# Preparing attention two pairs ahead, with tiny gate matmuls, a three-matmul inverse DFT and v by a plain DMA, in a fused attention and Hyena kernel

## The chip, the cores and the metric

The kernel runs on one core of a Trainium2 chip. The metric is the device time of one execution in microseconds (us). All runs quoted are fast runs, unless a run is called slow. The engines of a profile are PE (TensorE, matmuls), PEld (weight loads of PE), DVE (VectorE), ACT (ScalarE), POOL (GpSimd) and SP (the engine that issues most DMAs here). In the profile's lines L193 is line 193 of that kernel, x6 means six instructions, and `out<-in` names what is written and read. The granted clock is the share of PE's full clock that PE got; "half clock" is a stretch at 0.50.

## The reference

Block-sparse attention (4 batches, 8 heads, 768 positions, 64 numbers per head), and then a Hyena block on its output. Cut to what matters:

```python
# attention: each query sees its own 64-block and the 3 blocks with the best gate score, causally
k_rep = k.reshape(B, H, 12, 64, D).mean(axis=3)
gate_scores = einsum('bhsd,bhnd->bhsn', q, k_rep)      # causal blocks only
sel = top3(gate_scores) | own_block
attn = softmax(where(sel & causal, q @ k.T / sqrt(D), -1e9))
x = (attn @ v) as [B, S, 512]
# Hyena block
x1, x2, x3 = split(x @ w_proj)                          # 512 -> 3 * 512
conv = irfft(rfft(x2) * rfft(filter_fft))               # along the 768 positions
out = (x1 * conv * x3) @ w_out
```

## The kernel before

Heads are taken in pairs, four pairs in a batch. For each pair a *preparation* transposes q and k (`qp`, `kp`), forms the block means of k (`ks`), the gate scores and from them a mask (`ms`), and copies the parts by DMA into the operands `Qt` and `Kt` of the score matmuls. The mask lies in rows 64 to 75 of `Qt`, so a score can't start before the mask's DMA has landed. Attention of batch b runs together with the Hyena block of batch b−1. The Hyena block of the last batch runs alone, which this text calls the tail.

Loads and preparation of one pair:

```python
def load_v(st, j):                 # POOL issues it; the DMA converts fp32 to fp16
    for t in range(2):
        nc.gpsimd.dma_start(st["va"][:, :, 2 * j + t, 0:D], v_r[st["b"], :, :, 2 * j + t, :])

def pair_gen(st, j):
    ...  # qp -> q2h, q2l ; Qt[0:64] by DMA ; kp -> k2, ks ; Kt[0:64] by DMA
    for t in range(2):             # block means as a sum of two fp16 numbers
        nc.vector.tensor_copy(kmh[i][r, j, cc], ks[r, :])
        nc.vector.tensor_tensor(kml[i][r, j, cc], ks[r, :], kmh[i][r, j, cc], op=ALU.subtract)
```

Gates: wide matmuls with the means as weights, a copy by ACT, and fp32 transposes back.

```python
def gate_gen(st, j0, jn):          # batch 0: pair by pair; later batches: four pairs at once
    for part in range(2):
        for (wt, src) in ((kmh, q2h), (kml, q2h), (kmh, q2l), (kml, q2l)):
            for j in range(j0, j0 + jn):
                nc.tensor.matmul(gt[32*j:32*j+32, 0:w], lhsT=wt[:, j, :], rhs=src[:, j, P+p0:P+p0+w], ...)
        nc.scalar.copy(gts[gr, p0:p0 + w], gt[gr, 0:w])
    ...                            # transposes gts -> gn, top 3, mask nm, mt, ms
    nc.sync.dma_start(Qt[...][64:76, h % 2, P:S], ms[...])
```

Filter, frequency product and inverse DFT:

```python
def filter_gen():                  # runs within batch 0
    nc.gpsimd.dma_start(wp, ...); nc.gpsimd.dma_start(wo, ...)     # weights
    yield from trig_back()
    ...                            # six loads f0, f1 by SP, then fe = f0 + f1 (POOL), fo = f0 - f1 (DVE)

# in hyena_gen, for each block c of frequencies:
nc.gpsimd.tensor_sub(Y[:, c, 0, :], t1, t2)
nc.gpsimd.tensor_add(Y[:, c, 1, :], t3, t4)
# inverse DFT, for each dc and parity: two matmuls of 128 rows and two of 64
terms = [(Y[:, par, kk, ds_], G[:, 2 * par + kk, :]) for kk in range(2)]
terms += [(Y[r, 2, kk, ds_], G[r, 4 + kk, :]) for kk in range(2)]    # r: 64 rows
```

Order of the work: pair 0 is prepared first, and the instruction streams are then merged by weight.

```python
load_qk(st, 0); load_qk(st, 1)
for j in range(NP): load_v(st, j)
merge([first_pair, trig_gen])
# batch 0: attention, pairs 1..3, filter, and all four pairs of batch 1
# batch 1, 2: attention, Hyena of the batch before, all four pairs of the next batch
# batch 3: attention, Hyena ; then the tail
```

The softmax here doesn't subtract the row's maximum and nothing guards it: scores larger than these inputs give would overflow.

Of the kernel before, what the change touches and what calls it, by code (L numbers as in the profile page):

```python
# [17 lines left out]
def kernel(  # L18
# [25 lines left out]
    MAGIC = float(2 ** 23)  # L44
    TWO_PI = 2.0 * math.pi
# [33 lines left out]
    nc.gpsimd.tensor_copy(id16, id32)  # L79

    NS = 6
    Kt, Qt, kmh, kml = [], [], [], []
    for i in range(NS):
        Kt.append(const.tile([P, 2, S], FP16, name=f"Kt{i}"))
        Qt.append(const.tile([P, 2, S], FP16, name=f"Qt{i}"))
    for i in range(2):
        kh_ = const.tile([P, NP, 32], FP16, name=f"kmh{i}")
        kl_ = const.tile([P, NP, 32], FP16, name=f"kml{i}")
        nc.gpsimd.memset(kh_, 0.0)
        nc.gpsimd.memset(kl_, 0.0)  # L90
        kmh.append(kh_)
        kml.append(kl_)
    for i in range(NS):
        nc.vector.memset(Qt[i][64:P, :, :], 0.0)
# [7 lines left out]
    nc.gpsimd.memset(rowv, 1.0)  # L102
    nc.gpsimd.iota(rowv[0:1, :], pattern=[[1, HS]], base=0, channel_multiplier=0,
                   allow_small_or_imprecise_dtypes=True)
    cv3 = colv.rearrange("p (g k n) -> p g k n", g=3, k=2)
    nc.gpsimd.memset(cv3[:, :, 0, :], COS)
    nc.gpsimd.memset(cv3[:, :, 1, :], SIN)
    nc.gpsimd.memset(colv[:, P:P + 1], COS)
    nc.gpsimd.iota(cv3[0:1, 0:2, :, :], pattern=[[1, 2], [0, 2], [2, P]], base=0, channel_multiplier=0,
                   allow_small_or_imprecise_dtypes=True)  # L110
    nc.gpsimd.iota(colv[0:1, 2 * 256:S], pattern=[[0, 2], [1, 2], [2, 64]], base=256, channel_multiplier=0,  # L111
                   allow_small_or_imprecise_dtypes=True)
    nc.gpsimd.memset(colv[0:1, P:P + 1], 384.0)


    eblk = const.tile([P, S], FP16)
    nc.gpsimd.memset(eblk, 0.0)
    nc.gpsimd.memset(eblk[64:76, :], EMASK)
    nc.gpsimd.affine_select(
        out=eblk[64:76, :], in_=eblk[64:76, :], compare_op=ALU.is_ge,  # L120
        fill=0.0, base=0, pattern=[[1, S]], channel_multiplier=-64)
    nc.gpsimd.affine_select(
        out=eblk[64:76, :], in_=eblk[64:76, :], compare_op=ALU.is_ge,
        fill=0.0, base=63, pattern=[[-1, S]], channel_multiplier=64)
# [40 lines left out]
    def dft_fwd(xe, xo, c, kind, pt):  # L165

        if c < 2:
            src = xe if c == 0 else xo
            col = 256 * c + 128 * kind
            for t in range(HC):  # L170
                nc.tensor.matmul(pt, lhsT=F[:, t, col:col + P], rhs=src[:, t, :],
                                 start=(t == 0), stop=(t == HC - 1))
        else:
            col = 512 + 128 * kind
            for t in range(HC):
                for r, src in ((0, xe), (64, xo)):
                    nc.tensor.matmul(pt[r:r + 64, :], lhsT=F[:, t, col + r:col + r + 64],
                                     rhs=src[:, t, :], start=(t == 0), stop=(t == HC - 1),
                                     skip_group_check=True)

    def filter_gen():
        nc.gpsimd.dma_start(wp, moe_w_proj.rearrange("(c p) n -> p c n", p=P))
        nc.gpsimd.dma_start(wo, moe_w_out.rearrange("(c p) n -> p c n", p=P))
        yield 0.1
# [11 lines left out]
        for t, (f0, f1) in enumerate(fs):  # L196
            nc.gpsimd.tensor_tensor(fe[:, t, :], f0, f1, op=ALU.add)
            nc.vector.tensor_tensor(fo[:, t, :], f0, f1, op=ALU.subtract)
            yield 0.3
        for c in range(HC):  # L200
# [12 lines left out]
    q_r = q.rearrange("b h (c p) d -> b p c h d", p=P)  # L213
    k_r = k.rearrange("b h (c p) d -> b p c h d", p=P)
    v_r = v.rearrange("b h (c p) d -> b p c h d", p=P)

    def prep_begin(b):
        va = gp.tile([P, NQ, H, 65], FP16, name="va", tag="va")
        q2h = gp.tile([P, NP, S], FP16, name="q2h", tag="q2h", bufs=1)
        q2l = gp.tile([P, NP, S], FP16, name="q2l", tag="q2l", bufs=1)  # L220
        return dict(b=b, i=b % 2, va=va, q2h=q2h, q2l=q2l)

    def load_qk(st, j):
        b = st["b"]
        qn = nat.tile([P, NQ, 2, D], FP32, name="qn", tag="qn")
        kn = nat.tile([P, NQ, 2, D], FP32, name="kn", tag="kn")
        for t in range(2):
            nc.sync.dma_start(qn[:, :, t, :], q_r[b, :, :, 2 * j + t, :])
        for t in range(2):
            nc.sync.dma_start(kn[:, :, t, :], k_r[b, :, :, 2 * j + t, :])  # L230
        st[("n", j)] = (qn, kn)

    def load_v(st, j):
        if j == 0:
            nc.gpsimd.memset(st["va"][:, :, :, 64:65], 1.0)
        for t in range(2):
            nc.gpsimd.dma_start(st["va"][:, :, 2 * j + t, 0:D], v_r[st["b"], :, :, 2 * j + t, :])  # L237

    def pair_gen(st, j):
        i = st["i"]  # L240
        sl = (NP * st["b"] + j) % NS
        qn, kn = st[("n", j)]
        q2h, q2l = st["q2h"], st["q2l"]
        for hf in range(2):
            cs = slice(HS * hf, HS * (hf + 1))
            qp = ms_tile("qp")
            for c in range(HC):
                nc.tensor.transpose(qp[:, P * c:P * (c + 1)], qn[:, HC * hf + c, :, :], id32)  # L248
            nc.scalar.activation(q2h[:, j, cs], qp[:, 0:HS], AF.Copy, bias=0.0, scale=QS)  # L249
            nc.vector.scalar_tensor_tensor(out=q2l[:, j, cs], in0=qp[:, 0:HS], scalar=QS,  # L250
                                           in1=q2h[:, j, cs], op0=ALU.mult, op1=ALU.subtract)
            yield 0.33
        for t in range(2):
            nc.sync.dma_start(Qt[sl][0:64, t, :], q2h[64 * t:64 * t + 64, j, :])
        k2 = qkT.tile([P, S], FP16, name="k2", tag="k2")
        ks = qkT.tile([P, NB], FP32, name="ks", tag="ks")
        for hf in range(2):
            cs = slice(HS * hf, HS * (hf + 1))
            kp = ms_tile("kp")
            for c in range(HC):  # L260
                nc.tensor.transpose(kp[:, P * c:P * (c + 1)], kn[:, HC * hf + c, :, :], id32)  # L261
            nc.scalar.copy(k2[:, cs], kp[:, 0:HS])  # L262
            nc.vector.reduce_sum(ks[:, 6 * hf:6 * hf + 6],  # L263
                                 kp[:, 0:HS].rearrange("p (n t) -> p n t", t=64), axis=AX.X)
            yield 0.33
        for t in range(2):
            nc.sync.dma_start(Kt[sl][0:64, t, :], k2[64 * t:64 * t + 64, :])
        for t in range(2):
            r = slice(64 * t, 64 * t + 64)
            cc = slice(12 * t, 12 * t + 12)  # L270
            nc.vector.tensor_copy(kmh[i][r, j, cc], ks[r, :])
            nc.vector.tensor_tensor(kml[i][r, j, cc], ks[r, :], kmh[i][r, j, cc], op=ALU.subtract)

    W5 = S - P
    GW = (384, 256)

    def gate_gen(st, j0, jn):
        i = st["i"]
        q2h, q2l = st["q2h"], st["q2l"]
        gr = slice(32 * j0, 32 * (j0 + jn))  # L280
        hs = slice(2 * j0, 2 * (j0 + jn))
        gts = gp.tile([P, W5], FP32, name="gts", tag="gts", bufs=1)
        for part in range(2):
            p0, w = 384 * part, GW[part]
            gt = ms_tile("gt")
            n_ = 0
            for (wt, src) in ((kmh[i], q2h), (kml[i], q2h), (kmh[i], q2l), (kml[i], q2l)):
                for j in range(j0, j0 + jn):
                    nc.tensor.matmul(gt[32 * j:32 * j + 32, 0:w], lhsT=wt[:, j, :],  # L289
                                     rhs=src[:, j, P + p0:P + p0 + w],  # L290
                                     start=(n_ == 0), stop=(n_ == 3), skip_group_check=True)
                n_ += 1
            nc.scalar.copy(gts[gr, p0:p0 + w], gt[gr, 0:w])
            yield 0.8
        m8 = gp.tile([P, 5, H, 8], FP32, name="m8", tag="m8")
        nm = gp.tile([P, 5, H, NB], FP16, name="nm", tag="nm")
        for part in range(2):
            c0, cn = (1, 3) if part == 0 else (4, 2)
            gn = ms_tile("gn")
            for c in range(c0, c0 + cn):  # L300
                o = P * (c - c0)
                nc.tensor.transpose(gn[:, o + 32 * j0:o + 32 * (j0 + jn)],
                                    gts[gr, P * (c - 1):P * c], id32[gr, gr])

            gnh = gn.tensor

            def gap(p0, pn, c, cn_, n0, nn, cs=0):

                aps = [[512, pn]]
                if cn_ > 1:  # L310
                    aps.append([P + cs, cn_])
                aps += [[32, jn], [12, 2]]
                if nn > 1:
                    aps.append([1, nn])
                return bass.AP(tensor=gnh, offset=p0 * 512 + P * (c - c0) + 32 * j0 + n0, ap=aps)

            nc.vector.memset(gap(0, 64, c0, cn, 2 * c0 + 1, 1, cs=2), NEG)
            if part == 0:
                nc.vector.memset(gap(0, P, 1, 1, 4, 8), NEG)
# [239 lines left out]
    if True:  # L559
# [51 lines left out]
        for _ in hyena_gen(prev):  # L611
            pass
# [30 lines left out]
```

## Time and profile before

The median is 326.01 us in 3 runs (323.42 to 327.32). The profiled execution has a span of 325.2 us from its first to its last instruction.

The page's slices of the kernel before follow. Each digit is the busy share in one of 40 equal slices, in tenths; PEclk is the granted TensorE clock in tenths; DMA is the mean busy share of the 16 DMA engines.

```profile
PE   3613379687594797899889998999899999899984
PEclk9999998899978999999999999999999999999999
DMA  8999996166669945572009973200230000130005
```

PE has little to do in the first slices, while the DMA engines are busy. After slice 14 PE is nearly full.

The table of busy time by stretch follows, with cuts that I set at the first exp activation of each batch and at the last of all: start, batches 0 to 3, tail, and then the 18 us from 11 to 29 us alone. The columns are: from and to, length, busy time of each engine (with the number of instructions), granted clock, DMA share and GB/s. The DMA share adds up the times of the packets, so it can pass 1 where they overlap.

```profile
0.00:39.69 39.69, 14.08 (x52) 7.62 (x53) 27.65 (x77) 11.63 (x20) 27.10 (x48) 1.00 1.41 201
39.69:111.56 71.87, 54.24 (x480) 35.09 (x479) 39.94 (x203) 40.32 (x66) 16.74 (x33) 0.91 0.83 130
111.56:171.40 59.84, 53.52 (x486) 30.68 (x485) 42.63 (x137) 36.41 (x60) 24.84 (x36) 1.00 0.37 84
171.40:234.30 62.90, 58.65 (x516) 33.76 (x515) 42.52 (x141) 39.89 (x67) 30.77 (x42) 1.00 0.50 91
234.30:280.15 45.85, 45.38 (x388) 24.46 (x386) 26.04 (x53) 31.28 (x45) 22.99 (x33) 1.00 0.10 35
280.15:325.20 45.05, 37.13 (x219) 17.02 (x219) 18.13 (x35) 15.79 (x31) 15.91 (x12) 1.00 0.19 71
11.00:29.00 18.00, 5.99 (x24) 2.96 (x25) 15.33 (x53) 4.45 (x9) 9.05 (x11) 1.00 1.57 206
```

Three regimes are to be seen. In the start (39.7 us) PE works for 14.1 us. In batch 0 PE is busy for 54.2 of 71.9 us. From batch 1 on PE is busy for 89%, 93%, 99% and 82% of the stretch. The line for 11 to 29 us: PE and ACT have little to do there, but the DMA engines move 206 GB/s.

The chain of waits of the kernel before shows why attention starts so late (start, length, what; SPq is SP issuing):

```profile
14.55 3.94 SPq L193
...
19.01 13.72 DMA f_748<-in_moe_filter_fft_dram
...
33.93 4.63 DMA Qt_99<-ms
...
38.61 1.89 PE sp L385 x6
```

A filter load takes 13.7 us, DVE waits for it in `x2o`, the mask copy `ms` is queued behind that, the mask's DMA takes 4.6 us, and the first score `sp` runs at 38.61 us. Later in batch 0 the chain passes through a mask DMA twice more, for 4.3 us at 80.0 and for 3.2 us at 107.6.

Groups of instructions of the kernel before (line, engine, operation, out<-in, forms, count | busy us, mean ns | idle before, and what ended it):

```profile
L511 PE MATMUL cv<-G,Y 128*128 128x384 f16 x64 | 15.7, 327 | 0.7 <-POOL Y L484 0.5
L511 PE MATMUL cv<-G,Y 64*128 64x384 f16 x64 | 15.5, 328 | 0.7 <-POOL Y L484 0.5 <-POOL Y L483 0.2
```

The inverse DFT's matmul takes 328 ns with 64 rows of contraction and 327 ns with 128. Issuing the converting DMAs for v keeps POOL for another 26.9 us (32 issues).

### The profile page before, as it was taken

The numbers are of one execution on the slowest core, as the hardware profiler recorded it, in microseconds if no ns is written. First come the engines' busy times: TensorE is split into PE (matmuls) and PEld (weight loads), VectorE is DVE, ScalarE is ACT, GpSimd is POOL, SyncE is SP. The second block draws the span as 40 slices with busy tenths as digits, with TensorE's granted clock in tenths as the row PEclk, the third lists the DMA queues.
The fourth block names the chain that finished last, engine by engine and source line by source line (L and its number), as shares of the span: only waits on it lengthen the run. The fifth ranks groups of instructions, "written<-read, shape, count | busy, mean of one in ns | idle before, by whom it ended". The sixth has DMA issues, their size and how long they took to land.

```text
span 325.2 us, 6030 instructions
## 1 busy us (share of the span) xinstructions
PE 263.0 (81%) x2134; PEld 148.6 (46%) x2134; DVE 196.9 (61%) x644; ACT 175.3 (54%) x285; POOL 138.3 (43%) x202
## 2 busy tenths in 40 slices
PE   3613379687594797899889998999899999899984
PEld 2202145554362363555444645554455555444431
DVE  7992434768448059977642699685508765429530
ACT  2522367386650595555728866465485666461324
POOL 8924821110118126623339284244216754308540
PEclk9999998899978999999999999999999999999999
DMA  8999996166669945572009973200230000130005
GB/s 172 229 174 245 180 135 133 20 149 145 148 150 185 74 108 139 131 170 40 1 18 240 155 156 84 48 3 6 85 123 1 2 0 2 73 123 1 0 2 194
DMA packets 86558, 32.87 MB, mean 101 GB/s; under 512 B 77184, under 2 KB 82176, under 8 KB 86528
## 3 DMA queue, kind: packets, MB, share of 16 engines
q1 hardware_dynamic: 60384, 27.24, 35.5%
q0 software_dynamic: 26144, 5.25, 20.1%
q8 instruction: 17, 0.28, 0.3%
q14 instruction: 13, 0.11, 0.1%
HBM read 24.64 MB, written 6.29 MB: 95 GB/s over the span
## 4 chain that ended last, share of the span: by engine, by line
PE 53%; DVE 14%; DMA 11%; ACT 8%; POOL 6%; issue 4%; SPq 2%; POOLq 1%; ACTq 0%; DVEq 0%
PE x13p L495 9%; PE sp L385 8%; PE x2p L464 5%; PE cv L511 5%; PE po L403 5%; ACT ex L389 5%; DMA f_748<-in_moe_filter_fft_dram 4%; PE op L524 3%; PE kp L261 3%; PE qp L248 3%; PE gt L289 3%; POOL yT L519 2%; DVE ks L263 2%; PE xp L423 2%; DMA qn<-in_q_dram 2%
## 5 line engine op out<-in xcount | busy, mean ns | idle before, releaser
L389 ACT ACTIVATE ex<-sp 128x1024 f16<-128x1024 f32 (+1 forms) x96 | 85.9, 924 | 27.6 <-PE sp L385 26.8
L391 POOL TENSOR_SCALAR_AFFINE_SELECT ex<-ex 128x256 f16<-128x256 f16 x96 | 39.8, 417 | 114.4 <-ACT ex L389 114.4
L495 PE MATMUL x13p<-xT,wp 128*128 128x384 f16 x256 | 49.0, 326 | 1.7 <-ACT x_2170 L501 0.6
L519 POOL TENSOR_TENSOR yT<-prod,sd 128x768 f16<-128x768 f32 x16 | 29.0, 1810 | 28.2 <-DVE sd L518 25.3
L403 PEld LDWEIGHTS <-ex 128*128 128x128 f16 x672 | 30.8, 99 | 15.4 <-issue 7.6
L403 PE MATMUL po<-va,ex 128*128 128x65 f16 x672 | 36.0, 196 | 1.7 <-PE qp L248 1.5
L495 PEld LDWEIGHTS <-wp 128*128 128x128 f16 x256 | 23.6, 98 | 17.5 <-issue 4.9
L250 DVE SCALAR_TENSOR_TENSOR q2l<-qp,q2h 128x384 f16<-128x384 f32 x32 | 17.2, 550 | 23.0 <-ACT q2h L249 22.6
L511 PE MATMUL cv<-G,Y 128*128 128x384 f16 (+1 forms) x128 | 28.9, 327 | 1.4 <-POOL Y L484 0.9
L249 ACT ACTIVATE q2h<-qp 128x384 f16<-128x384 f32 x32 | 15.7, 496 | 23.0 <-PE qp L248 22.6
L237 POOL DMA_DIRECT2D va<-in_v_dram x32 | 26.9, 861 | 0.0
L524 PE MATMUL op<-wo,yT 128*128 128x512 f16 x96 | 23.2, 380 | 3.9 <-POOL yT L519 3.9
L261 PE MATMUL kp<-id_91,kn 128*128 128x128 f32 x96 | 19.5, 327 | 6.3 <-DVE ms L345 3.4
L248 PE MATMUL qp<-id_91,qn 128*128 128x128 f32 x96 | 18.8, 320 | 7.0 <-DMA qn<-in_q_dram 5.1
L527 ACT COPY osb<-op 128x512 f32<-128x512 f32 x24 | 13.4, 590 | 20.1 <-PE op L524 18.7
L263 DVE TENSOR_REDUCE ks<-kp 128x6 f32<-128x384 f32 x32 | 17.4, 552 | 6.4 <-ACT k_1063 L262 3.8
L415 DVE TENSOR_TENSOR xn<-po,rec 128x384 f16<-128x384 f32 x32 | 17.8, 555 | 0.7
L261 PEld LDWEIGHTS kp<-id_91,kn 128*128 128x128 f32 x96 | 13.0, 167 | 11.2 <-DVE ms L345 3.8
L248 PEld LDWEIGHTS qp<-id_91,qn 128*128 128x128 f32 x96 | 12.6, 161 | 12.0 <-POOL colv L111 5.1
L411 DVE RECIPROCAL rec<-po 128x6 f32<-128x6 f32 x32 | 6.1, 189 | 19.0 <-PE po L403 18.5
L517 DVE TENSOR_TENSOR sd<-ce,cv 128x384 f32<-128x384 f32 x16 | 8.8, 552 | 13.5 <-PE cv L511 11.4
L511 PEld LDWEIGHTS <-Y 128*128 128x128 f16 (+1 forms) x128 | 9.0, 96 | 15.4 <-issue 11.4
(297 smaller groups left out, 489.6 us busy)
## 6 DMA issues: line engine op xcount, KB each, us to landing
qn<-in_q_dram SPq DMA_DIRECT2D x32, 192.0 KB
kn<-in_k_dram SPq DMA_DIRECT2D x32, 192.0 KB
out_dram<-osb SPq DMA_DIRECT2D x24, 256.0 KB
va<-in_v_dram POOLq DMA_DIRECT2D x32, 96.0 KB, 6.2
wp<-in_moe_w_proj_dram POOLq DMA_DIRECT2D x1, 1536.0 KB, 18.9
Qt_99<-q2h SPq DMA_DIRECT2D x6, 96.0 KB
Qt_101<-q2h SPq DMA_DIRECT2D x6, 96.0 KB
Qt_103<-q2h SPq DMA_DIRECT2D x6, 96.0 KB
```

Of the source, the lines that this page charges most:

```text
L237: nc.gpsimd.dma_start(st["va"][:, :, 2 * j + t, 0:D], v_r[st["b"], :, :, 2 * j + t, :])
L248: nc.tensor.transpose(qp[:, P * c:P * (c + 1)], qn[:, HC * hf + c, :, :], id32)
L261: nc.tensor.transpose(kp[:, P * c:P * (c + 1)], kn[:, HC * hf + c, :, :], id32)
L263: nc.vector.reduce_sum(ks[:, 6 * hf:6 * hf + 6], kp[:, 0:HS].rearrange("p (n t) -> p n t", t=64), axis=AX.X)
L385: nc.tensor.matmul(sp[:, col:col + w], lhsT=kt[:, P * kc:P * (kc + 1)], rhs=qt[:, q0:q0 + w], start=True, stop=True, skip_group_check=True)
L389: nc.scalar.activation(ex[:, 0:w], sp[:, 0:w], AF.Exp, scale=ESC)
L391: nc.gpsimd.affine_select(out=dv, in_=dv, compare_op=ALU.is_ge, fill=0.0, base=0, pattern=[[0, 2], [1, P]], channel_multiplier=-1)
L403: nc.tensor.matmul(po[:, 65 * c:65 * c + 65], lhsT=exs[pi][:, col:col + P], rhs=st["va"][:, kc, h, :], start=(kc == 0), stop=(kc == c), sk ...
L495: nc.tensor.matmul(xp[:, 0:HS], lhsT=wp[:, d2, base + P * dc:base + P * (dc + 1)], rhs=xT[:, d2, hs:hs + HS], start=(d2 == 0), stop=(d2 == ...
L511: nc.tensor.matmul(cv[:, 0:HS], lhsT=lh, rhs=rh, start=(n_ == 0), stop=(n_ == 3))
L519: nc.gpsimd.tensor_mul(yT[:, dc, :], prod, sd)
L524: nc.tensor.matmul(op, lhsT=yT[:, d2, P * c:P * (c + 1)], rhs=wo[:, d2, :], start=(d2 == 0), stop=(d2 == DC - 1))
```

## The change

It has five parts: prepare each pair by itself, two pairs ahead of its attention, from the start to the end of the kernel; compute gate scores directly in their natural layout by tiny matmuls; fold the two 64-row terms of the inverse DFT into one of 128 rows; load v as fp32 by a plain DMA from SP and cast it on POOL; and move small set-up work between engines. Cut to its core:

```diff
+    load_qk(0); load_v(0); load_qk(1); load_v(1)
+    merge([Stream(prep_gen(0), ...), Stream(trig_gen(), ...), Stream(prep_gen(1), ...)])
+    for sl in range(2, NS): fill_kt(sl)
+    def later_preps(b):
+        for j in range(NP):
+            g = NP * b + j + AHEAD                  # AHEAD = 2
+            if g < NG:
+                if g + 1 < NG: load_qk(g + 1); load_v(g + 1)
+                yield from prep_gen(g)
+    load_qk(AHEAD); load_v(AHEAD)                   # after the merge above
     ...
-    # gate_gen: wide matmuls, ACT copy, fp32 transposes
+        for c in range(1, NQ):
+            for n_, (qx, w) in enumerate(((q2h, 0), (q2h, 1), (q2l, 0), (q2l, 1))):
+                nc.tensor.matmul(gn[:, 32 * c:32 * c + 24], lhsT=qx[:, P * c:P * (c + 1)],
+                                 rhs=km[:, w, 0:24], start=(n_ == 0), stop=(n_ == 3))
     ...
-        Y = hy.tile([P, HC, 2, Dm], FP16, name="Y", tag="Y")
+        Y = hy.tile([P, 6, Dm], FP16, name="Y", tag="Y")
-            nc.gpsimd.tensor_sub(Y[:, c, 0, :], t1, t2)
-            nc.gpsimd.tensor_add(Y[:, c, 1, :], t3, t4)
+            if c < 2: ...                           # as before
+            else:
+                for par in range(2):
+                    r = slice(64 * par, 64 * par + 64)
+                    nc.gpsimd.tensor_sub(Y[0:64, 3 * par + 2, :], t1[r, :], t2[r, :])
+                    nc.gpsimd.tensor_add(Y[64:P, 3 * par + 2, :], t3[r, :], t4[r, :])
     ...
-                for n_, (lh, rh) in enumerate(terms):                          # 4 terms
+                for n_, g_ in enumerate((2 * par, 2 * par + 1, 4 + par)):      # 3 terms
     ...
-        nc.gpsimd.dma_start(st["va"][...], v_r[...])
+        nc.sync.dma_start(vn, v_r[:, n, :])         # later, on POOL: va = vn in fp16
     ...
+        # filter_gen: the weight loads now come after the filter loads
```

The diff has a sixth part: the changed kernel builds its whole schedule under `tc.manual_schedule(engines={SP, Pool})`, which the kernel before does not. In the changed kernel SP follows the program text, which has the loads of pair 2 after the masks of pairs 0 and 1, and the six filter loads within batch 0. In the kernel before the text has the filter within batch 0, but its trace shows the six loads issued from 6.7 to 19.4 us, in the start.

## The prediction

> **What bounds the kernel now.** The page's slices and a table of busy time by stretch show three regimes. 0–38.6 us: no attention; PE 13.0 us busy, DVE 27.7. 38.6–110 us (batch 0 with seven pair preparations and the filter): PE 77%, ACT 56%, DVE 56%; granted clock 0.90. 110–283 us: PE 88%, 94%, 97%, PE-bound. 283–325 us: the last hyena alone, PE 83%. In the chain of waits the first score waits for a mask DMA (33.9–38.6 us), which waits for a DVE mask copy queued behind a filter operand still loading (19.0–32.7 us). Later scores of batch 0 again wait 4.3 and 3.2 us for a mask DMA: the just-in-time chain transpose, means, gate, mask, DMA, score is exposed.
>
> **What changes, costed from the trace.**
> 1. Start. Only pairs 0 and 1 are prepared before attention; filter loads come later; v is not queued four pairs deep. The new start should be DVE-bound: mask memsets (six of 0.8 us), 18 trig operations (0.35–0.55 us), two preparations, block-row copies; the instruction order puts pair 0's mask copy after nearly all of it. Estimate: first score at 31 us instead of 38.6: −7.5 us.
> 2. Batch 0. Four preparations (pairs 2–5) instead of seven, two pairs ahead, so no score waits for a mask. PE work about 36–40 us, ACT about 34, DVE about 41. Estimate 47 us instead of 71: −24 us. Partly this moves work: two preparations (2 × 3.8 us PE) go to batch 3, whose PE is full: +6 us. Together −18.
> 3. Inverse DFT: 4 matmuls to 3 for each of 32 accumulations. The 64-row and 128-row forms take 328 and 327 ns, and eight take about 1.6 us in the chain, 0.2 us each; so 32 × 0.2–0.27 = 6–8 us less PE. This agrees with the Trainium skill, "TensorE: Matmul & The Clock Gate", LDWEIGHTS section: rows of the contraction don't matter. About 7 us of it is critical. Price: for the third Y block four 64-row Pool operations instead of two (each 1.27 us here, set by free size, so +2.5 us per batch); hidden under attention, but in the tail the six Pool operations are on the chain, so the tail gets no faster (41–42 us).
> 4. Gates: per batch, 32 wide matmuls, 5 fp32 transposes and their ACT copies become 80 tiny matmuls in natural layout. Before about 2.5 us PE per batch; after 80 × 30–55 ns = 2.4–4.4 us. DVE: about +0.8 us per pair. Net +2 us on PE.
> 5. v: Pool loses 26.9 us of DMA issue, gains 16 casts of about 1.1 us. Pool isn't the bottleneck: about 0.
>
> Sum: 326 − 7.5 − 18 − 7 + 2 = **about 295 us**, range **281 to 307**. Chances: faster 0.97, same 0.025, slower 0.005.
>
> **What would show it.** First score near 31 us; batch 0's exp activations spanning 45–50 us; no score waiting over 1 us for a mask DMA after the first; later stretches of about 60, 60, 53 us with PE at least 92% busy; tail 40–42 us with Pool's Y operations in the chain; 96 cv matmuls; no Pool DMA issue for v.
>
> **What would make it wrong.** Tiny matmuls costing near 0.1 us each (+16 us PE); SP in program order delaying loads, so that pair 2 is late (42–44 us); DVE saturating batch 0; start much shorter if DVE work overlaps better; Pool's partition-shifted Y operations slower than 1.27 us.

## The result, and the profile after

The changed kernel takes 308.89 us (median of 4 runs, 307.46 to 309.96); the kernel before took 326.66 us in the same rounds (median of 4; one of them, 328.45 us, counts as slow, and the three fast ones have the median 326.01). The ratio is 0.9485, with a 95% interval of 0.9394 to 0.9575. A ratio here is always the mean time of one kernel's fast runs over that of the kernel before in the same rounds, so it isn't quite the ratio of the medians. The direction was predicted, but the time lies outside the predicted range of 281 to 307 us.

The page's slices after:

```profile
PE   3364687399689989897999898989997999897883
PEclk9999999759799999999999999999999999999799
DMA  9920978999939370909593909094931100400005
```

The third and fourth DMA digits are now 2 and 0: the engines are idle there. In slices 5 to 13 nearly all of them are 7 to 9. PEclk falls to 7 and 5 in slices 8 and 9.

The table by stretch after, with the cuts again at the first and last exp of each batch, and 11 to 29 us last:

```profile
0.00:29.79 29.79, 13.19 (x84) 7.93 (x85) 25.26 (x92) 15.33 (x23) 5.73 (x17) 1.00 0.59 107
29.79:82.49 52.70, 37.56 (x407) 25.32 (x406) 31.29 (x119) 29.71 (x45) 21.43 (x39) 0.89 1.01 197
82.49:143.04 60.55, 54.37 (x550) 34.57 (x549) 47.56 (x152) 37.46 (x60) 30.26 (x44) 0.98 0.58 113
143.04:205.84 62.80, 57.23 (x569) 35.75 (x566) 49.04 (x157) 39.46 (x66) 30.24 (x44) 1.00 0.61 129
205.84:260.55 54.71, 51.48 (x498) 31.35 (x495) 39.36 (x125) 36.10 (x57) 26.39 (x38) 1.00 0.34 80
260.55:307.70 47.15, 37.36 (x210) 18.18 (x208) 18.73 (x37) 15.91 (x31) 19.41 (x14) 0.95 0.18 67
11.00:29.00 18.00, 9.37 (x69) 5.19 (x70) 16.83 (x71) 8.93 (x15) 0.91 (x1) 1.00 0.30 62
```

The differences, with the prediction put into the same stretches:

| stretch | before | after | measured | predicted |
|---|---|---|---|---|
| start | 39.7 | 29.8 | −9.9 | −7.5 |
| batch 0 | 71.9 | 52.7 | −19.2 | −24 |
| batches 1 and 2 | 122.7 | 123.4 | +0.6 | together +1: |
| batch 3 | 45.9 | 54.7 | +8.9 | two preparations +6, |
| tail | 45.0 | 47.1 | +2.1 | inverse DFT −7, gates +2 |
| sum | 325.2 | 307.7 | −17.5 | −30.5 |

The last column is the prediction's sum; where it listed stretches it had 60, 60 and 53 us for batches 1 to 3, against 60.6, 62.8 and 54.7. So the start gave more than predicted. Batch 0 gave 4.8 us less, and the later stretches together cost 11.6 us (0.6 + 8.9 + 2.1) where 1 was predicted.

The chain of waits after, in batch 0 (pieces from three places):

```profile
30.54 3.62 DMA kn<-in_k_dram
...
53.10 0.57 SPq L191
...
53.72 3.76 DMA f_727<-in_moe_filter_fft_dram
...
75.56 5.19 DMA Qt_108<-ms
```

Pair 2's k is only issued at 30.04 us and lands at 34.16 us, after attention has begun. A filter load is issued at 53.1 us, the first of six. POOL is the engine that waits for it, and `ex`, the causal masking of exponentials that POOL does for attention, comes behind it. At 75.56 us a score waits again for a mask's DMA, 5.2 us; the prediction said that no score would wait over 1 us for one.

The timeline after, at that place (start, length, instruction, idle time before it and its releaser):

```profile
57.62 1.77 POOL L196 TENSOR_TENSOR x2e<-f_726,f_727 128x512 f16<-128x512 f32 x1 [11.89 <-DMA f_727<-in_moe_filter_fft_dram]
59.34 0.86 POOL L351 TENSOR_SCALAR_AFFINE_SELECT ex<-ex 128x256 f16<-128x256 f16 x1
59.44 0.59 PE L172 MATMUL hf<-x2e,F 128*128 128x512 f16 x1 [4.97 <-POOL x2e L196]
```

POOL stands still for 11.9 us, PE for 4.97 us, and the granted clock is 0.50 from 57.6 to 67.8 us. This agrees with the Trainium skill, "TensorE: Matmul & The Clock Gate", section "HAM oscillation — how this bites in real kernels", which warns of idle gaps of PE longer than about 3.4 us.

The group after that answers to those of before (columns as there):

```profile
L475 PE MATMUL cv<-G,Y 128*128 128x384 f16 x96 | 21.2, 339 | 3.0 <-POOL Y L451 2.6 <-POOL Y L446 0.5
```

There are 96 `cv` matmuls for 128, as predicted, and their idle time before grew from 1.4 us to 3.0 us, nearly all of it waits for POOL's `Y`. For v, POOL has 14.5 us of casts in place of 26.9 us of issue.

The timeline after, early in the tail:

```profile
281.81 1.26 POOL L451 TENSOR_TENSOR Y<-t_4503,t_4492 64x512 f16<-64x512 f32 x1
283.12 0.34 PE L475 MATMUL cv<-G,Y 128*128 128x384 f16 x1 [0.91 <-POOL Y L451]
...
284.46 1.26 POOL L451 TENSOR_TENSOR Y<-t_4503,t_4492 64x512 f16<-64x512 f32 x1
285.78 0.34 PE L475 MATMUL cv<-G,Y 128*128 128x384 f16 x1 [1.67 <-POOL Y L451]
...
286.89 2.13 PE L475 MATMUL cv<-G,Y 128*128 128x384 f16 x6
```

A 64-row operation of POOL takes 1.26 us, as long as one of 128 rows did before. PE waits for two of the four, and then runs six `cv` matmuls in 2.13 us at half clock.

The half clock doesn't follow from these waits alone. e9 and e12 below have the same code in the tail, and the same two waits, but no half clock there. In e9:

```profile
278.35 0.34 PE L481 MATMUL cv<-G,Y 128*128 128x384 f16 x1 [1.68 <-POOL Y L457]
279.18 1.14 PE L481 MATMUL cv<-G,Y 128*128 128x384 f16 x6
```

Their tails take 45.5 us (mean granted clock 0.99 and 0.98), against 47.1 us (0.95) in the profiled run of the changed kernel. So of the 2.1 us by which the tail grew, some 1.7 are this stretch of half clock, which came in some kernels with this tail and not in others.

### The profile page after: what moved, and what is told of

It reads as the page before. It is cut to its first block, busy times and chain, and to the rows that moved or that the text cites. A ratio compares the mean times of both kernels' runs of the same rounds, so it can differ in the third digit from the quotient of the medians.

```text
span 307.7 us, 6418 instructions
## 1 busy us (share of the span) xinstructions
PE 251.2 (82%) x2304; PEld 153.1 (50%) x2304; DVE 211.2 (69%) x678; ACT 174.0 (57%) x277; POOL 133.5 (43%) x196
## 4 chain that ended last, share of the span: by engine, by line
PE 51%; DVE 25%; ACT 6%; POOL 6%; DMA 5%; issue 4%; SPq 1%; POOLq 1%; ACTq 0%; DVEq 0%
PE sp L345 8%; PE x13p L462 8%; PE x2p L425 6%; PE cv L475 4%; PE po L364 4%; PE op L489 4%; ACT ex L349 3%; POOL yT L484 3%; DVE ks L257 3%; PE gn L282 2%; PE kp L256 2%; DVE q2l L275 2%; DMA Qt_108<-ms 2%; PE xb L172 2%; PE xa L172 2%
## 5 line engine op out<-in xcount | busy, mean ns | idle before, releaser
L462 PE MATMUL x13p<-xT,wp 128*128 128x384 f16 x256 | 51.5, 329 | 2.5 <-DVE prod L470 1.9
L364 PEld LDWEIGHTS <-ex 128*128 128x128 f16 x672 | 33.2, 100 | 20.2 <-POOL ex L351 9.7
L364 PE MATMUL po<-va,ex 128*128 128x65 f16 x672 | 38.2, 197 | 2.5 <-POOL ex L351 2.2
L256 PE MATMUL kp<-id_91,kn 128*128 128x128 f32 x96 | 19.2, 319 | 7.9 <-DMA kn<-in_k_dram 7.3
L257 DVE TENSOR_REDUCE ks<-kp 128x6 f32<-128x384 f32 x32 | 17.5, 549 | 11.6 <-PE kp L256 11.5
L475 PE MATMUL cv<-G,Y 128*128 128x384 f16 x96 | 21.2, 339 | 3.0 <-POOL Y L451 2.6
L273 PE MATMUL qp<-id_91,qn 128*128 128x128 f32 x96 | 17.8, 302 | 2.1 <-ACT k_263 L259 0.7
L256 PEld LDWEIGHTS kp<-id_91,kn 128*128 128x128 f32 x96 | 12.1, 160 | 12.7 <-POOL rowv L111 4.5
L240 POOL TENSOR_SCALAR_AFFINE_SELECT va<-vn 128x768 f16<-128x768 f32 x16 | 14.5, 906 | 6.3 <-DMA vn<-in_v_dram 6.3
L489 PEld LDWEIGHTS <-yT 128*128 128x128 f16 x96 | 8.7, 97 | 14.6 <-POOL yT L484 5.7
L282 PEld LDWEIGHTS <-q2h 128*128 128x128 f16 x160 | 10.2, 98 | 9.0 <-issue 5.6
L320 DVE COPY ms<-mt 24x640 f16<-24x640 f16 x16 | 7.6, 477 | 10.0 <-PE mt L317 10.0
```

The source lines that it names most:

```text
L256: nc.tensor.transpose(kp[:, P * c:P * (c + 1)], kn[:, HC * hf + c, :, :], id32)
L257: nc.vector.reduce_sum(ks[:, 6 * hf:6 * hf + 6], kp[:, 0:HS].rearrange("p (n t) -> p n t", t=64), axis=AX.X)
L273: nc.tensor.transpose(qp[:, P * c:P * (c + 1)], qn[:, HC * hf + c, :, :], id32)
L364: nc.tensor.matmul(po[:, 65 * c:65 * c + 65], lhsT=exs[pi][:, col:col + P], rhs=va[:, h % 2, kc, :], start=(kc == 0), stop=(kc == c), skip ...
L462: nc.tensor.matmul(xp[:, 0:HS], lhsT=wp[:, d2, base + P * dc:base + P * (dc + 1)], rhs=xT[:, d2, hs:hs + HS], start=(d2 == 0), stop=(d2 == ...
L475: nc.tensor.matmul(cv[:, 0:HS], lhsT=Y[:, 3 * par + n_, ds_], rhs=G[:, g_, :], start=(n_ == 0), stop=(n_ == 2))
```

## The experiments

Two theories stood at the outset for the missing gain in batch 0.

- **Loads.** The change starts attention earlier by leaving out loads, and those loads now fall into batch 0, where they delay k, the filter, q and the masks. Then moving loads back into the idle DMA time of 11 to 29 us must shorten batch 0, with its computing unchanged.
- **Computing (the rival).** Batch 0 has more work on PE, DVE or ACT than I had counted (tiny matmuls, casts). Then moving loads does little.

For the later stretches the candidates were: moved preparations, a smaller gain from the inverse DFT, POOL's `Y` in the tail, and collisions of DVE with POOL. All edits are against the changed kernel, unless said otherwise. All kernels gave correct results. For times quoted without an interval, the table at the end of this section has it.

### e1_filter_early: issue the filter's loads earlier in batch 0

```diff
     def filter_gen():
-        yield from trig_back()
         fe, fo, and six loads ...
         yield 0.1
+        yield from trig_back()
```

> The changed kernel with one move: the six filter loads are queued at the start of the filter's stream, before the transposes of the DFT matrix, so about 10 us earlier. Theory A (batch 0 loses its time to a stall: Pool, in program order, waited 11.9 us for a filter operand with the masking of finished exps queued behind it; the PE fell idle for 5 us from 54.5 us, and its granted clock was 0.5 for the next 10 us): Pool's wait falls below 3 us, no stretch of half clock after it, 301 to 304 us instead of 309. Theory B (batch 0 is limited by the sum of its work on DVE, ACT and PE, and the stall only moved waiting that was due anyway): 307 to 310 us.

Measured: 304.96 us. Batch 0 fell only from 52.7 to 50.8 us. POOL's wait shrank from 11.9 to 2.3 us, but the chain of waits of this run has a new wait in its place:

```profile
61.05 14.25 DMA qn<-in_q_dram
...
75.43 0.53 PE qp L273 x3
```

The load of q for a later pair takes 14.25 us. What follows: the wait of POOL was one place where late loads were felt. With that place gone, the next load became the wait, while 199 GB/s moved throughout batch 0. The other 3.3 us of the gain in the profiled run are in batch 1 (57.3 for 60.6 us), and they belong together: the stretch of batch 0 now holds 27 more matmuls (434 for 407) and that of batch 1 25 fewer (525 for 550). So the stall was a real part of the loss, about 4 us, with nearly the same bytes in batch 0 (199 GB/s × 50.82 us = 10.1 MB for 10.4). The result lies between what theory A (301 to 304) and theory B (307 to 310) expected.

### e7_pair2_early, e9_pair2_filter_early, e10_all_loads_early: move loads out of batch 0, step by step

e7 issues pair 2's loads before the first merge, with a third buffer so that nothing need be waited for. e9 does this and issues the six filter loads there too. e10 does all of e9, and issues the four weight loads from POOL before batch 0.

```diff
-    nat = ctx.enter_context(tc.tile_pool(name="nat", bufs=2))
+    nat = ctx.enter_context(tc.tile_pool(name="nat", bufs=3))
         load_qk(1); load_v(1)
+        load_qk(AHEAD); load_v(AHEAD)               # e7, e9, e10
+        filter_load()                               # e9, e10
         merge([...])
         for sl in range(2, NS): fill_kt(sl)
+        four weight DMAs on gpsimd                  # e10
-        load_qk(AHEAD); load_v(AHEAD)
```

> The changed kernel with a third buffer for the fp32 inputs, so that pair 2's q, k and v are queued right behind pairs 0 and 1, at about 8 us, instead of behind their masks at 30 us. From 11 to 29 us the changed kernel's DMA engines are nearly idle, and in batch 0 their share is 1.01 (197 GB/s). Theory C (batch 0 is now bounded by DMA, because work that before was loaded during the start is now loaded in it): 1.2 MB moved out of batch 0 at 197 GB/s is 6 us; batch 0 shrinks by 4 to 6 us and the total is 303 to 305. Theory B (batch 0 is bounded by its engines): only the PE's 2.7 us wait for k of pair 2 goes, or nothing: 307 to 309.

> As e7_pair2_early, and the filter's six loads (1.6 MB) are also queued at the start, behind pair 2's. Theory C: another 1.6 MB / 197 GB/s = 8 us of DMA time leaves batch 0, and Pool never waits for the filter, so no half clock in batch 0 either: 299 to 302 us, first score no later than 31 us. If the early loads delay the first mask instead, the first score moves to 33 us or later and the total gains little: 304 or more.

> As e9_pair2_filter_early, and the two weight matrices (4.2 MB read) are queued on Pool after the second cast of v, at about 14 us, instead of in batch 0. Theory C says DMA in batch 0 falls well below full (share under 0.8), but the first masks now queue behind the weights as they did before the change: first score at 33 to 38 us, batch 0 shorter by as much; total 298 to 304, within 2 us of e9_pair2_filter_early.

Measured: 303.76, 299.39 and 298.75 us. The table by stretch of e9 (start, batch 0, and 11 to 29 us):

```profile
0.00:32.30 32.30, 16.31 (x98) 10.51 (x99) 28.83 (x101) 16.57 (x26) 5.74 (x17) 1.00 0.93 189
32.30:74.50 42.20, 32.13 (x392) 22.55 (x392) 26.78 (x111) 28.47 (x42) 20.19 (x39) 0.89 0.93 171
11.00:29.00 18.00, 10.61 (x76) 6.54 (x77) 17.29 (x71) 8.09 (x15) 0.91 (x1) 1.00 0.98 216
```

and of e10 (start and batch 0):

```profile
0.00:37.14 37.14, 15.31 (x93) 9.71 (x94) 29.76 (x102) 16.67 (x27) 8.86 (x21) 1.00 1.14 223
37.14:71.13 33.99, 30.80 (x398) 21.41 (x396) 23.96 (x104) 28.41 (x41) 17.02 (x35) 1.00 0.72 143
```

Batch 0 has nearly the same matmuls in the changed kernel and in e7, e9 and e10 (407, 396, 392, 398), but shrinks with the bytes that move in it. The bytes are the rate times the length of the stretch:

| kernel | MB in batch 0 | length of batch 0, us | start and batch 0 together, us |
|---|---|---|---|
| e5 (below) | 189 GB/s × 60.57 us = 11.4 | 60.6 | 90.5 |
| after | 197 × 52.70 = 10.4 | 52.7 | 82.5 |
| e7 | 203 × 46.53 = 9.4 | 46.5 | 78.7 |
| e9 | 171 × 42.20 = 7.2 | 42.2 | 74.5 |
| e10 | 143 × 33.99 = 4.9 | 34.0 | 71.1 |

What follows: the rival is refuted as the cause of batch 0's length. Nearly the same matmuls fit in 34.0 us, when fewer bytes move beside them. Nor is it the half clock: batch 0 of e9 has the same mean granted clock as the changed kernel (0.89) and is 10.5 us shorter. (That e9 would have no half clock in batch 0 had been expected, and was wrong.) (A part of DVE's work, 15 of 119 instructions in e10, moved to the start with pair 2, so the comparison holds for PE and ACT more strictly than for DVE. DVE was busy for 31.3 of 52.7 us in the changed kernel, so it was not full either.) Loading is the main limit of batch 0 in the changed kernel; e1 shows that the order of the loads counts beside their bytes. Moving loads into the idle 11 to 29 us pays: in e9 the start grew by 2.5 us and batch 0 shrank by 10.5.

e10 shows the limit of this. Its first exp came at 37.1 us, because the weights, issued from POOL, and the masks, issued from SP, share the DMA engines. Its chain of waits has these pieces:

```profile
19.82 11.25 DMA Kt<-k
...
31.14 4.91 DMA Qt<-ms
```

An on-chip copy of k takes 11.25 us there. This agrees with the Trainium skill, "Trainium Kernel Development and Optimization", section "Key Constraints": DMAs issued from different engines run on the same 16 DMA engines and interleave. e10 is not told apart from e9 (0.9097 to 0.9211 and 0.9111 to 0.9208): what batch 0 won further (8.2 us) was lost again in the start (4.8 us) and batch 1 (1.0). Another 1.4 us are in the tail, whose code is the same in both: e10 has the stretch of half clock there (0.95), e9 doesn't (0.99).

### e5_ahead4: prepare four pairs ahead instead of two

```diff
-    AHEAD = 2
+    AHEAD = 4          # batch 0 prepares six pairs (2 to 7), batch 3 none
```

> The changed kernel, preparing four pairs ahead instead of two: two pairs still come before the first score, but batch 0 then prepares six pairs instead of four, and batch 3 none instead of two. Theory moved work (the two preparations in batch 3 cost all of the 8.9 us by which that batch grew, because its PE is full, and batch 0 has idle engines to take them): batch 3's exps span 46 us instead of 54.7, batch 0 grows by under 4 us, total 304 to 306 us. Rival (the same work costs the same anywhere, batch 0 is as full): batch 0 grows by 8 or 9 us, total 308 to 311.

Measured: 318.3 us, more than either theory had expected. Batch 3 shrank from 54.7 to 49.1 us, so two preparations there cost 5.6 us; the prediction had 6. But batch 0 grew to 60.6 us and batch 1 from 60.6 to 68.1 us. What follows: two pairs ahead is better than four for this kernel (three wasn't run), and the prediction's price for two preparations in batch 3 was right. Batch 0's growth fits the table of bytes above. Batch 1's growth of 7.5 us isn't settled: 9.0 MB move in it (132 GB/s × 68.11 us) for 6.8 in the changed kernel (113 × 60.55), and DVE has 5.7 us more to do, but no run separates the two.

### e2_old_idft: the inverse DFT as before

```diff
-        Y = hy.tile([P, 6, Dm], ...)          # and three matmuls of 128 rows
+        Y = hy.tile([P, HC, 2, Dm], ...)      # and two of 128 and two of 64 rows, as before
```

> The changed kernel with the inverse DFT of before: four matmuls per accumulation, two of them with 64 rows, two full-height Pool operations per batch for the third block instead of four half-height ones. My prediction says the new form saves 0.2 to 0.27 us of PE for each of 32 accumulations, 7 us of it critical: so this kernel would take about 315 us (314 to 317). The rival: the PE time saved is lost again to Pool's two extra operations per batch, in the tail above all, and to waits on Pool: 307 to 310 us.

Measured: 312.49 us, so the new form is worth about 3.6 us (312.49 − 308.89) where the prediction had 7. The intervals of the two ratios just overlap (0.9546 to 0.9584, and 0.9394 to 0.9575 for the changed kernel), so the size rests on the stretches too: batches 1, 2 and 3 were each 0.6 to 1.1 us longer with the old form (61.2, 63.8 and 55.8 us), and the tail was 0.8 us shorter (46.3). That last difference isn't a price of the new form: this tail has no stretch of half clock (0.99), and the new form without one took 45.5 us in e9 and e12, less than the 46.3 here, though with three `op` matmuls fewer in the stretch (45 for 48). What follows: the direction was right, at half the size; 312.49 us also lies between the 314 to 317 us expected and the rival's 307 to 310. In batches 1 to 3 a part of the saved time of PE isn't critical, and in the tail no clear gain or loss is left.

### e3_tail_dve: in the tail, let DVE make the third block of Y

```diff
-                    nc.gpsimd.tensor_sub(Y[0:64, ...], ...); nc.gpsimd.tensor_add(Y[64:P, ...], ...)
+                    eng = nc.vector if tail["on"] else nc.gpsimd
+                    eng.tensor_sub(Y[0:64, ...], ...); eng.tensor_add(Y[64:P, ...], ...)
```

> The changed kernel, but in the last hyena alone (nothing beside it) the four half-height operations for the third block of Y run on DVE instead of Pool. Theory A (the four 1.26 us Pool operations are on the chain in the tail, where the PE waited 0.9 and 1.7 us for them and then got half clock for 3.4 us): tail from the last exp to the end falls from 47 to 43 or 44 us, total 305 to 306. Theory B (the tail is bounded by its matmuls; the PE's gaps there were filled later): within 1 us of 309.

Measured: 305.45 us, and the tail takes 43.7 us for 47.1. Its timeline, at the place that answers to that of the changed kernel:

```profile
282.13 0.69 DVE L452 TENSOR_TENSOR Y<-t,t 64x512 f16<-64x512 f32 x1
282.88 0.34 PE L476 MATMUL cv<-G,Y 128*128 128x384 f16 x1
...
284.11 1.14 PE L476 MATMUL cv<-G,Y 128*128 128x384 f16 x6
```

DVE takes 0.67 to 0.69 us where POOL took 1.26. No wait stands ahead of the last `cv`, and six of them take 1.14 us at full clock, not 2.13. What follows: the four operations of POOL, together with the half clock that came after the waits for them, cost the tail 3.4 us in the profiled run. The tails of e9 and e12, with POOL's form at full clock (45.5 us), divide it: about 1.7 us are POOL's operations (45.5 − 43.7), and 1.7 the half clock (47.1 − 45.5), which doesn't always come.

### e4_v_as_before: v by the converting DMA that POOL issues

```diff
-        nc.sync.dma_start(vn, v_r[:, n, :])   # and cast_v on POOL
+        for t in range(2):
+            nc.gpsimd.dma_start(va[:, t, :, 0:D], v_r[:, n:n + NQ, :])
```

> The changed kernel with v loaded as before: a converting DMA issued by Pool straight into the fp16 tile, two for each pair, no cast on Pool. My prediction gave v's part about 0: 308 to 310 us here too. Rival 1 (the Pool cast, 0.91 us each, collides with DVE and with the masking of exps): faster, 305 to 307. Rival 2 (issuing costs Pool 0.86 us twice per pair[...], in front of masking): slower, 311 to 314.

Measured: 311.44 us (three fast runs), 2.6 us above the changed kernel by the medians, with intervals that overlap (0.9489 to 0.9565). This is in the range that rival 2 had (311 to 314), but the new way of v is at best a small gain, and not a shown one. The profiled run of this kernel was slow (599.28 us) and isn't used; see the last section.

### e6_old_gate: the old form of the gate, pair by pair

```diff
-        for c in range(1, NQ):                 # 20 tiny matmuls
-            ... matmul(gn[:, 32*c:32*c+24], lhsT=qx[:, P*c:P*(c+1)], rhs=km[:, w, 0:24])
+        for p0, w_ in ((0, 384), (384, 256)):  # 8 wide matmuls, 2 copies by ACT
+            ... matmul(gt[0:32, 0:w_], lhsT=km[:, w, :], rhs=qx[:, P+p0:P+p0+w_])
+            nc.scalar.copy(gts[:, p0:p0 + w_], gt[0:32, 0:w_])
+        for c in range(1, NQ):                 # 5 fp32 transposes
+            nc.tensor.transpose(gn[:, 32*c:32*c+32], gts[:, P*(c-1):P*c], id32[0:32, 0:32])
```

> The changed kernel with the gate as before, but for one pair at a time: eight wide matmuls (32 by 384 or 256), two ACT copies to SBUF and five fp32 transposes in place of the 20 tiny matmuls. In the changed kernel's trace tiny matmuls follow each other every 27 ns: 0.55 us of PE for a pair, against about 1.1 for the wide ones and 0.4 for the transposes: 16 x 0.95 = 15 us more PE, of which two thirds are on the chain: 317 to 321 us. My prediction took the new gate for 2 us dearer in all than the old one of four pairs at once; were a tiny matmul as dear as I feared (55 ns or more with its weight load), this kernel would take 309 to 313.

Measured: 333.44 us (three fast runs), 24.6 us more than the changed kernel, and no gain over the kernel before (1.0126 to 1.0291). This was a miss: 317 to 321 us had been expected. The start grew by 4.2 us, batches 0 to 3 by 1.6, 6.1, 6.5 and 5.1 us. In the records of this run 128 wide matmuls of 320 ns, 80 transposes of 238 ns and 32 copies of 411 ns on ACT stand for 320 tiny matmuls. In the changed kernel the tiny matmuls follow each other every 27 ns (timeline, pairs of two):

```profile
13.46 0.21 PE L282 MATMUL gn<-kmb_110,q2h 128*128 128x24 f16 x2
13.51 0.21 PE L282 MATMUL gn<-kmb_110,q2l 128*128 128x24 f16 x2
```

So a pair's 20 cost some 0.55 us of PE. What follows: of the two gates tried, only the tiny matmuls make preparing pair by pair affordable. The prediction priced them against the old gate that took four pairs at once, at 2.4 to 4.4 us for a batch and +2 us net on PE. At 27 ns a batch's 80 take 2.2 us, less than the 2.5 it gave for the old gate, so by this estimate that term was too dear.

### e12_means_cast_act: cast the block means on ACT

```diff
-            nc.vector.tensor_copy(km[r, 0, cc], ks[r, :])
+            nc.scalar.copy(km[r, 0, cc], ks[r, :])
```

This tests the collision of DVE with POOL. The timeline of the changed kernel shows two casts of 64x12 numbers that together span 2.3 us, beside two operations of POOL:

```profile
140.28 1.80 POOL L484 TENSOR_TENSOR yT<-prod,sd 128x768 f16<-128x768 f32 x1 [0.56 <-DVE sd L483]
...
140.70 2.31 DVE L264 CAST kmb_110<-ks 64x12 f16<-64x12 f32 x2
...
142.08 0.91 POOL L240 TENSOR_SCALAR_AFFINE_SELECT va<-vn 128x768 f16<-128x768 f32 x1
```

Where no operation of POOL runs beside it, such a cast takes 0.15 to 0.17 us in this trace. The Trainium skill, "SBUF — State Buffer", section "Who interferes with whom", says that DVE and GpSimd share one pair of ports as an exclusive lock, that a cast may take it, and that ACT shares no port. The trace agrees: POOL's two operations end at 142.08 and 142.99 us, and the two casts together at 143.01.

> The changed kernel with the 32 casts of the key means (64 by 12) on ACT instead of DVE. Without a running Pool operation such a cast takes 0.18 us on DVE, but in the changed kernel 13.5 us in all, up to 1.4 us while Pool runs a 1.81 us product. Theory L (these blocked casts, and what queues behind them on DVE, are why batches 1 to 3 did not get shorter although their PE work fell): batches 1 and 2 take 59 to 61 us instead of 60.6 and 62.8, total 304 to 306. Rival (the collisions hit operations with slack, or the next DVE operation is blocked in their place): within 1 us of 309.

Measured: 305.5 us, 3.4 us less; the interval (0.9327 to 0.9438) overlaps that of the changed kernel. A cast takes 198 ns on ACT. Batches 1, 2 and 3 fell by 0.9, 1.2 and 0.3 us. In the profiled run, which is this kernel's fastest, batch 0 fell by 1.6 us too, and the tail by 1.7, but the tail has no such cast: there only the half clock is missing. The collision partly moved to the next instructions of DVE: the subtraction that follows took 10.1 us in all, for 8.1. What follows: the collisions are real, and cost something like 2 us in batches 1 to 3; the total gain is likely, but not settled.

### e13_loads_tail and e14_three_repairs: the repairs together

e13 is e9 with e3; e14 is e13 with e12.

> The two repairs together: pair 2 and the filter queued at the start (299.4 us alone) and the tail's third block of Y on DVE (305.4 alone, 3.4 less than the changed kernel). They are in different stretches, so they should add: 299.4 - 3.4 = 296 us (295 to 297). If this comes out, the prediction's 295 us is met once the two new waits are gone, and what is left of the error lies in terms that cancel.

> The loads of pair 2 and the filter at the start, the tail's third block of Y on DVE, and the casts of the key means on ACT, all three on the changed kernel. Theory: the first removes the DMA-bound part of batch 0, the second Pool from the tail's chain, the third DVE's blocked casts in batches 1 to 3; they lie in different stretches, so the third's 3.4 us come off the 297.8 us of the first two: 294 to 295.5 us, batches 1 and 2 about 59.5 and 61.6 us. Rival: what the third gave alone came from batch 0 and from the tail, which are shortened already: 297 to 298.

Measured: 297.45 us (three fast runs) and 295.86 us (six runs). e13 gained 1.9 us over e9 where 3.4 had been expected. That fits a tail that in e9's profiled run had no half clock to lose (45.5 us, and 43.7 in e14); e13's own profiled run was slow, so its tail isn't seen. The last repair isn't told apart from noise (0.9075 to 0.9148, and 0.9022 to 0.9103). e14 is the fastest kernel: 0.9063 of the kernel before, and by the medians 13 us faster than the change as it was given. Its first exp comes at 31.8 us, batch 0 takes 42.8 us and the tail 43.7.

### All runs

| kernel | median, us (fast runs) | ratio to before | 95% interval |
|---|---|---|---|
| the change as given | 308.89 | 0.9485 | 0.9394 to 0.9575 |
| e1_filter_early | 304.96 | 0.9342 | 0.9317 to 0.9368 |
| e2_old_idft | 312.49 | 0.9565 | 0.9546 to 0.9584 |
| e3_tail_dve | 305.45 | 0.9349 | 0.9328 to 0.9371 |
| e4_v_as_before | 311.44 | 0.9527 | 0.9489 to 0.9565 |
| e5_ahead4 | 318.3 | 0.9744 | 0.9705 to 0.9783 |
| e6_old_gate | 333.44 | 1.0209 | 1.0126 to 1.0291 |
| e7_pair2_early | 303.76 | 0.9287 | 0.9228 to 0.9346 |
| e9_pair2_filter_early | 299.39 | 0.916 | 0.9111 to 0.9208 |
| e10_all_loads_early | 298.75 | 0.9154 | 0.9097 to 0.9211 |
| e12_means_cast_act | 305.5 | 0.9382 | 0.9327 to 0.9438 |
| e13_loads_tail | 297.45 | 0.9112 | 0.9075 to 0.9148 |
| e14_three_repairs | 295.86 | 0.9063 | 0.9022 to 0.9103 |

The medians leave out one slow run each of e4, e6 and e13. The kernel before had medians of 326.2 to 327.01 us beside these runs.

## Why the prediction was wrong

**Right.** The direction; the cause of the late start (first score at 28.74 us, 31 predicted, 38.61 before; as predicted, DVE bounds the new start: it is busy for 25.3 of the 29.8 us, and copies the first mask at 26.2); the price of two preparations in batch 3 (5.6 us in e5, 6 predicted); that 64-row and 128-row matmuls take the same time; that POOL's `Y` is on the chain in the tail.

**The step that failed, in batch 0.** The prediction put it so: "Four preparations (pairs 2–5) instead of seven, two pairs ahead, so no score waits for a mask. ... Estimate 47 us instead of 71: −24 us." It measured 52.7, −19.2. The estimate summed the busy time of PE, ACT and DVE. It didn't count bytes, and a score did wait for a mask (5.2 us at 75.56). In the kernel before, the DMA engines loaded ahead in the long start, at 206 GB/s from 11 to 29 us; in the changed kernel they moved 62 GB/s there, because SP issues pair 2's loads only after the masks of pairs 0 and 1 (the inputs have two buffers; e7 had to add a third to move them). Those loads, the filter and the weights came into batch 0: 10.4 MB at 197 GB/s. e7, e9 and e10 show that the length of batch 0 follows these bytes with the same matmuls, down to 34.0 us. The estimate of the computing was therefore not too low; a different resource was the limit. The prediction named "SP in program order delaying loads, so that pair 2 is late" as a risk (42 to 44 us); its k did land late, at 34.2 us, but the risk was not in the sum.

**The terms that were mis-sized in the later stretches.** There +1 was predicted and +11.6 measured, so this is the larger part of the miss of 13 us between the two sums.

- The inverse DFT, "About 7 us of it is critical": 3.6 by the medians of e2, with intervals that just overlap. That is 3.4 us of the miss.
- The tail: "the six Pool operations are on the chain, so the tail gets no faster". In the profiled run it got 2.1 us slower. Some 1.7 of these are a stretch of half clock that the prediction didn't think of; without it (e9, e12) the tail takes 45.5 us for 45.0 before, so "no faster" was nearly right. e3 shows that POOL's form costs about 1.7 us there at full clock, which DVE can save.
- The gates and DVE: the prediction had "DVE: about +0.8 us per pair" and didn't let it cost anything. The busy time of DVE grew from 42.6 to 47.6 us in batch 1 and from 42.5 to 49.0 in batch 2. e12 indicates about 2.4 us for one kind of collision with POOL in batches 1 to 3 (0.9 + 1.2 + 0.3).
- The two preparations that "go to batch 3, whose PE is full: +6 us": the preparations are as predicted, but the stretch grew by 8.9 us although the inverse DFT takes about 1 us off it. The counts of instructions say that it also holds five more `op` and six more `po` matmuls, which lay in neighbouring stretches before, and it holds its own gates. How the remaining 3 to 4 us divide isn't settled.

These terms come from different kernels and overlap, so they aren't to be added up to the exact difference. What the repairs show together is firmer: e13, which repairs only the loads and the tail, takes 297.45 us and lies near the 295 that was predicted, for reasons which the prediction didn't have in its sum.

**v.** Predicted about 0; the new way reads 2.6 us better in e4, with overlapping intervals. Not decided.

## What to carry to other kernels

When a change makes a start-up phase shorter, ask what was being loaded in it: the bytes don't go away, and in the next phase they stand in front of the small DMAs that work waits for. Cost a stretch by bytes as well as by each engine's busy time, and compare DMA share in idle stretches before and after. Read the granted clock beside every stretch that you compare: here 1.7 us of a tail came and went with it under the same code. An operation with half the partitions need not be half as long (POOL: 1.26 us for 64 rows and for 128); and where an engine works in program order, a wait for a load also holds up the unrelated work queued behind it.

## What the Trainium skill lacked or had wrong

- "TensorE: Matmul & The Clock Gate", section "HAM oscillation — how this bites in real kernels", gives idle gaps over about 3.4 us as what brings the half clock. In the tail of the changed kernel no gap that the trace shows passed 1.7 us, but from 286.3 to 289.7 us the granted clock was 0.50. The page's next section does tell of short idle times that bring the half clock, but gives no number. In the 3.4 us ahead of the stretch (282.9 to 286.3) PE was busy for 1.51 us. That isn't enough by itself: in e9 PE was busy for 1.53 us from 275.5 to 278.9, in the same place of the tail, and the clock stayed full. No run fixes the threshold.
- The same section draws, for its example, about 1.67 us throttled for each long wait. The half-clock stretches in the two kernels lasted 3.4 us (four in the kernel before) or 10.2 us (after a gap of 4.97 us), which are one and three of the windows of about 3.4 us that its section "What's actually happening" names.
- The same page, section "LDWEIGHTS (loading the stationary operand)", says that rows of the contraction don't matter for a weight load, and its formula (columns over 1.2) gives an estimate of 107 ns for 128 columns. The trace agrees on rows (94 ns for the loads of 64 rows of `Y` in the kernel before, 97 ns for 128), and the loads of the tiny gate matmuls took 98 ns. The page gives no measured spacing for fp16 matmuls of 24 columns with a load each: here they follow every 27 ns, so the records of the loads overlap several deep. The floor of about 25 ns in its section "Back-to-back issue gap" fits that, while the text there, that load and matmul together set the spacing, would lead one to expect more.
- Two profiled runs, of e4 (599.28 us) and e13 (810.32 us), were in a state in which only PE is slow, while the three other runs of each took 310.48 to 311.5 us and 297.12 to 298.2. In e13 this group had a mean of 900 ns, for 329 ns in the changed kernel:

```profile
L469 PE MATMUL x13p<-xT,wp 128*128 128x384 f16 x256 | 171.9, 900 | 0.6 <-ACT ce L486 0.6
```

  DVE's `xT` (558 ns, for 554) was as ever. Both traces hold no record of the clock at all: their pages have no PEclk line, and the 1.0 that is listed for them is only what stands where nothing was recorded. So whether the clock was low is not known, and the cause is open. The first page above has a warning, section "Seeing it yourself", that clock records can be unreliable, but no page read says how to tell such a run. It must not be compared with others.
- "SBUF — State Buffer", section "Who interferes with whom", gives the rule of the shared ports, and the trace agrees. It gives no sizes for very small operations: here a cast of 64x12 numbers grew from 0.17 us to as much as 1.5 us beside an operation of POOL of 1.8 us. When the cast was taken away, the subtraction after it, which reads two operands from SBUF, took longer; the same section names that case too.
